# Attention followed by an RWKV channel mix: a new order of steps, tile products in groups, batch 0's query loaded in position halves, and GpSimd's loads held until phi has landed

## The chip, the cores and the metric

The kernel runs on one core of one Trainium2 chip. The metric is the device time of one execution in microseconds (us). A core has five engines with instruction streams of their own: TensorE (PE, matrix products; its weight loads are listed apart as PEld), VectorE (DVE), ScalarE (ACT), GpSimd (POOL) and SyncE (SP). Data come in and go out through DMA queues, into which ACT, POOL and SP put transfers. Engines wait for one another on semaphores.

## The reference

Eight batches of eight heads, 576 positions of 64 features, and 32 slots. Attention goes through the slots:

```python
a = exp(phi - max)                       # phi: 8 x 8 x 576 x 32
a = a / (sum(a, axis=2) + 1e-09)         # softmax over the positions
k_m = einsum('bhsm,bhsd->bhmd', a, k)
v_m = einsum('bhsm,bhsd->bhmd', a, v)
attn = softmax(scale * q @ k_m^T)        # over the 32 slots
attn_out = attn @ v_m
```

The heads are then put side by side (x: 8 x 576 x 512), and the channel mix follows, with 512 model and 1024 inner features:

```python
xk = mu_k * x + (1 - mu_k) * x_prev      # x_prev: x one position earlier
xr = mu_r * x + (1 - mu_r) * x_prev
k = maximum(xk @ w_k, 0)
out = sigmoid(xr @ w_r) * (k * k @ w_v)
```

## The kernel before

**An order written out by hand.** `PLAN` (lines 19 to 84) is a list of words that is executed from left to right (lines 785 to 798); each word issues the instructions of one step, so it fixes the order of every engine's stream. A word is `batch:step`, or `kind:name`. Digits behind `@` are the PSUM banks that the step takes, `/a` and `/d` put a step's copy or activation on ScalarE or VectorE. A step with `yield` in it is named several times, once for each of its parts: first the products, later the work on their result.

**Layout.** A partition's row holds nine neighbouring positions: a batch's q, k, v and phi lie as 128 partitions by (4 head pairs, 9, features), and partitions 0 to 63 hold one head of a pair, 64 to 127 the other. "Position j" below is one of these nine. Many products are tile products: 64 rows by 32 columns of TensorE's array or 32 by 64, so that several heads or pairs run beside each other, each with its own weight load; the others use the whole 128 by 128 array.

**Steps of a batch** (`attention`, names of the words in brackets): exponential of phi (`exp`), its sums over positions by a product with ones (`z`), products of that with k and v (`kv`, or `k`, `v`, and for batch 0 `kg0`, `kg1`, `vg0`, `vg1`, two head pairs each; line 315), normalizing (`nk`, `nv`, for batch 0 `h0`, `h1`; lines 340 and 342), transposing the key and value slots (`tk`, `vt`), transposing q on VectorE (`q0`, `q1`; `turn_q`), scores (`s`, line 401), their exponentials (`es..`), the sums over slots (batch 0: `l`, `r`, `y`, a product, a logarithm and an exponential with negative sign on ScalarE, then the weighing; other batches: a fold on VectorE, `fe`, `fs`, `fo`, and `w0`, `w1`).

**Two ways through the channel mix.** Batch 0 mixes first: `mub` brings mu into the tile `mu_m`, `nk0` to `nr1` (`norm_mu`) make the value slots times mu (the tile `vm`), `mk0`, `mk1`, `mr0`, `mr1` (tile products, `mixed`, line 358) make xk and xr for two ranges of positions (`FIRST`), `uk..`, `ur..` copy them out of PSUM (line 546), `c0:..` multiply with w_k (`key`, line 600), `g:0.` with w_r. Batches 1 to 7 multiply the value slots with the weights instead (`Gs`, `G0`: `project`, line 492; `Es`, `E0`: copies of 512 columns out of PSUM, line 498; `D`: a difference, line 501), with weights scaled by mu (`m:`, line 282 on), and the key products then run on attention's weights (`cN:`, `pair_key`, lines 618 to 626). Relu (`r:`) and square (`s:`) follow on ScalarE and VectorE, the gates (`g:`, `t:`), and the products with w_v (`o:`, `value`, lines 742 and 748) with the store (`store`).

**Fillers.** `b:NxM` (`keep_busy`, line 250) issues N products of zeros, 64 M columns wide, that nothing uses; `WARM` is such a call before the first step.

**Loads.** ScalarE's queue loads batch 0's phi (`load_phi`, line 168) and then k in two halves by head pairs (line 180), as f32; two casts each turn k into bf16 (`0:c..`, `cast_k`). Everything else is loaded by GpSimd (`preload`, the words `p:..`, converted on the way to bf16 where the tile has it), in program order: GpSimd waits at a word for the buffer to be free, and what stands behind it waits too. `PRE` lists what GpSimd does before the plan begins: `q:0g`, the first two head pairs of batch 0's query, then `id`, the identity matrix. `p:q:0h` brings the other two.

**Positions of batch 0.** `scores` works in two parts, `s0` for five of the nine position columns and `s1` for four. In the kernel before, `turn_q` puts position 8 into the first column and positions 0 to 7 behind it, two VectorE transposes for each two head pairs; `tokens` (lines 512 to 515) lists which columns `mixed` takes as now and as one position earlier, and `store` (line 708) where a column's tokens go in the output. `HALVES` are the five and the four columns.

Of the kernel before, what the change touches and what calls it, by code (L numbers as in the profile page):

```python
# [83 lines left out]
]  # L84

WARM = (78, 1)

PRE = "q:0g id:"
TAIL = ("o:71", "o:e3a", "o:e3b",)


NJ = 9
# [5 lines left out]
def kernel(  # L98
# [75 lines left out]
    def load_parity(dst, src, r):  # L174
        nc.gpsimd.dma_start(out=dst[r].rearrange("p h j d -> p h (j d)"), in_=rows(src)[r])
# [654 lines left out]
```

## Time and profile before

| what | value |
|---|---|
| time, median of 3 runs | 201.72 us (201.43 to 202.26) |
| the profiled execution | 201.73 us, span 199.8 us, mean granted clock 0.99 |
| VectorE busy | 159.6 us (80%) |
| ScalarE busy | 147.0 us (74%) |
| moved by DMA | 31.96 MB, mean 160 GB/s |
| instructions | 6543 |

The span goes from the first to the last instruction of the profiled execution. The page's views give, for each engine, its busy time and its share in 40 slices of the span; for each DMA queue what it carried; the chain of waits, which is followed back from the last instruction and tells at each moment what the end depended on (rows: start, length, engine, tile, line, number of instructions); and groups of instructions by line, engine and tile (tile written, tile read, shapes, count, busy time, mean ns). A number in square brackets in a timeline is the idle time ahead of an instruction, with what ended it. "issue" in the chain is time in which an engine waited for nothing that the profile shows. Views by window give the length of a stretch, then the busy time and number of TensorE's products, of its weight loads, and of DVE, ACT, POOL, SP, then the granted clock, the DMA share and GB/s.

### The profile page before, as it was taken

The page shows a single profiled execution, that of the slowest core. Times are in us where ns is not written, and L with a number is a line of the kernel's source. Part 1 is how long each engine was busy: PE and PEld are TensorE (multiplying, and loading weights), DVE is VectorE, ACT ScalarE, POOL GpSimd, SP SyncE. Part 2 cuts the span into 40 slices and gives each one's busy share as a digit, 9 for nine tenths or more (in the row PEclk, how much of TensorE's full clock was granted, in tenths as well). Part 3 has the DMA queues.
Part 4 walks back from the last instruction along what each step waited for, and adds up shares of the span by engine and source line. Part 5 has one row for each costly group of instructions (what it writes and reads, how often), then busy time and mean ns, then how long its engine had stood idle before and what let it go on. Part 6 is the DMA issues. An engine that isn't in the chain of part 4 may idle for free.

```text
span 199.8 us, 6543 instructions
## 1 busy us (share of the span) xinstructions
PE 185.4 (93%) x2655; PEld 105.9 (53%) x2676; DVE 159.6 (80%) x352; ACT 147.0 (74%) x350; POOL 29.3 (15%) x44
## 2 busy tenths in 40 slices
PE   8797999999999999799999999999999999999950
PEld 8443665478644457335645565356544663474430
DVE  2245599898988999699989998998989898996430
ACT  2337797889689688499998689898885799795310
POOL 7644323001240103203015000000000000000000
PEclk9999999999999999999999999999999999999996
DMA  5999999999999992999919999034012411032242
GB/s 203 274 204 259 212 207 199 248 229 290 279 209 213 227 321 35 175 268 262 228 22 190 218 248 206 1 98 117 5 53 55 125 37 41 11 89 74 77 114 75
DMA packets 26174, 31.96 MB, mean 160 GB/s; under 512 B 3096, under 2 KB 20768, under 8 KB 26144
## 3 DMA queue, kind: packets, MB, share of 16 engines
q0 software_dynamic: 17376, 20.32, 55.6%
q1 hardware_dynamic: 7408, 9.19, 16.1%
q10 hardware_dynamic: 1360, 2.03, 3.1%
q8 instruction: 21, 0.34, 0.7%
q14 instruction: 9, 0.07, 0.1%
HBM read 38.28 MB, written 9.44 MB: 239 GB/s over the span
## 4 chain that ended last, share of the span: by engine, by line
PE 77%; DVE 7%; ACT 4%; DMA 3%; issue 3%; SPq 1%; ACTq 1%; DVEq 0%
PE pv L748 25%; PE pk L618 7%; PE pk L626 6%; PE pb L626 6%; PE gps L492 5%; PE idle L250 4%; PE kvps L315 3%; PE pv L742 3%; PE pk L600 3%; DMA k0f<-in_k_dram 3%; PE pb L678 3%; PE pr L670 2%; PE pr L678 2%; DVE rl L586 2%; ACT G L498 2%
## 5 line engine op out<-in xcount | busy, mean ns | idle before, releaser
L748 PE MATMUL pv<-wv,sq 128*128 128x512 bf16 (+1 forms) x276 | 59.3, 355 | 1.1 <-issue 0.5
L498 ACT CAST G<-gps 128x512 bf16<-128x512 f32 x75 | 39.5, 620 | 7.6 <-PE gps L492 7.4
L748 PEld LDWEIGHTS <-sq 128*128 128x128 bf16 x288 | 26.8, 98 | 29.4 <-issue 4.3
L754 DVE SCALAR_TENSOR_TENSOR o<-sg,pv 128x512 f32<-128x512 f32 (+3 forms) x41 | 24.8, 616 | 9.8 <-PE pv L748 5.4
L626 PEld LDWEIGHTS <-G 128*128 128x128 bf16 x224 | 21.3, 97 | 8.0 <-issue 0.9
L626 PE MATMUL pk<-diff,G 128*128 128x288 bf16 x112 | 22.9, 286 | 0.0
L626 PE MATMUL pb<-diff,G 128*128 128x288 bf16 x112 | 22.9, 286 | 0.0
L592 DVE TENSOR_TENSOR sq<-rl 128x576 bf16<-128x576 bf16 (+2 forms) x49 | 20.7, 438 | 1.8 <-ACT rl L584 0.7
L622 ACT COPY pb<-pk 128x288 f32<-128x288 f32 x43 | 16.6, 397 | 6.2 <-PE pk L618 4.6
L618 PE MATMUL pk<-atn,G 128*128 128x288 bf16 x112 | 20.3, 286 | 0.1
L647 ACT ACTIVATE sg<-pr 128x512 f32<-128x512 f32 x22 | 13.1, 606 | 7.8 <-PE pr L700 4.0
L584 ACT ACTIVATE rl<-pk 128x288 bf16<-128x288 f32 (+2 forms) x39 | 16.0, 414 | 3.7 <-PE pk L626 2.0
L584 ACT ACTIVATE rl<-pb 128x288 bf16<-128x288 f32 x36 | 14.6, 421 | 3.5 <-PE pb L626 3.3
L250 PE MATMUL idle<-zeros 128*128 128x64 bf16 (+3 forms) x120 | 15.2, 277 | 1.2 <-DVE zeros L181 1.0
L586 DVE TENSOR_SCALAR rl<-pk 128x288 bf16<-128x288 f32 (+2 forms) x33 | 14.6, 449 | 0.7 <-PE pk L626 0.5
L465 DVE TENSOR_TENSOR atn<-e,lz 128x576 bf16<-128x576 bf16 (+2 forms) x18 | 12.1, 689 | 3.3 <-ACT lz L437 3.1
L501 DVE TENSOR_TENSOR G<-G 128x1024 bf16<-128x1024 bf16 x21 | 14.1, 685 | 0.6 <-ACT G L498 0.4
L618 PEld LDWEIGHTS <-G 128*128 128x128 bf16 x112 | 10.6, 98 | 5.5
L590 ACT ACTIVATE sq<-rl 128x576 bf16<-128x576 bf16 (+2 forms) x23 | 12.3, 559 | 0.4 <-DVE rl L586 0.3
L295 ACT ACTIVATE em<-ph 128x1152 bf16<-128x1152 f32 (+1 forms) x9 | 9.6, 1071 | 1.6 <-DMA ph<-in_phi_dram 1.6
L382 DVE STREAM_TRANSPOSE qT<-q 128x576 uint32<-128x576 uint32 x14 | 10.6, 766 | 0.0
L415 ACT ACTIVATE e<-scps 128x288 bf16<-128x288 f32 x28 | 9.4, 424 | 1.4 <-PE scps L401 1.4
(100 smaller groups left out, 279.2 us busy)
## 6 DMA issues: line engine op xcount, KB each, us to landing
out_dram<-o SPq DMA_DIRECT2D x134, 64.0 KB, 2.8
ph<-in_phi_dram POOLq DMA_DIRECT2D x7, 576.0 KB, 13.6
kv<-in_k_dram POOLq DMA_DIRECT2D x7, 576.0 KB, 14.4
q<-in_q_dram POOLq DMA_DIRECT2D x7, 576.0 KB, 15.4
kv<-in_v_dram POOLq DMA_DIRECT2D x7, 576.0 KB, 12.8
k0f<-in_k_dram ACTq DMA_DIRECT2D x2, 576.0 KB, 7.0
wv<-in_moe_w_v_dram POOLq DMA_DIRECT2D x2, 512.0 KB, 20.1
ph<-in_phi_dram ACTq DMA_DIRECT2D x1, 576.0 KB, 4.5
```

The costliest lines, as they stand in the source:

```text
L250: nc.tensor.matmul(ps.rearrange("p (a b) -> p a b", b=64), lhsT=zeros, rhs=zeros[:, :64].unsqueeze(1).to_broadcast([128, blocks, 64]), sta ...
L498: return lambda: copier()(g_tile()[:, v, c, GCOLS[i]], st["gps", v, i][c])
L501: return lambda: nc.vector.tensor_sub(g_tile()[:, 1, :, GCOLS[i]], g_tile()[:, 2, :, GCOLS[i]], g_tile()[:, 0, :, GCOLS[i]])
L584: nc.scalar.activation(rl, ps, AF.Relu, scale=HALF ** 0.5)
L586: nc.vector.tensor_scalar(rl, ps, 0.0, HALF ** 0.5, op0=AL.max, op1=AL.mult)
L592: nc.vector.tensor_mul(dst, rl, rl)
L618: nc.tensor.matmul(pa, lhsT=st["G"][:, 2, c, f], rhs=st["at"][:, c, :NP], start=c == 0, stop=False, skip_group_check=True)
L622: copier()(pb, pa)
L626: nc.tensor.matmul(ps, lhsT=st["G"][:, v, c, f], rhs=st["d"][:, kind, c], start=False, stop=c == 1, skip_group_check=True)
L647: nc.scalar.activation(gated[name], ps, AF.Tanh, scale=0.5)
L748: nc.tensor.matmul(pv[:, cols], lhsT=sq[:, fi, lo:lo + 128], rhs=wv_sb[:, fi, cols], start=(fi == 0), stop=(fi == NF - 1))
L754: nc.vector.scalar_tensor_tensor(o[:, cols], in0=gated[name][:, cols], scalar=1.0, in1=pv[:, cols], op0=AL.add, op1=AL.mult)
```

## The change

Four things change, in one diff.

- `PLAN` is a new order of the same steps, with other banks and some other engines for copies. Steps with tile products stand more often next to each other: from the first key product on, TensorE's stream changes between tile shapes 61 times where it did 71 times. The fillers are others: 78 of 64 columns, 30 of 512, 9 of 256, and one each of 320, 384 and 448 before; 46 of 512, 4 of 320, 2 of 384, one of 448 and one of 256 after. TensorE's stream has 5214 instructions in place of 5346. Of the copies of 512 columns (line 498) ScalarE has 76 and VectorE 8 (75 and 9 before); the four scalings of w_r go from VectorE to ScalarE.
- `PRE` becomes `id: after: q:0b`. `after` is a new step: GpSimd copies one element of batch 0's phi into the tile `mark`, so it and all that GpSimd loads behind it wait until phi has landed. `WARM` becomes ten fillers of 512 columns.
- Batch 0's query is loaded in position halves: `a` is the first five positions of all head pairs, `b` the other four. `load_parity` is gone. `turn_q` makes one transpose for each half, `q0` for five positions, `q1` for four, and leaves the positions in their order; `tokens` and `store` are adapted to that. `s1` (positions 5 to 8) now stands before `s0`. The first mixing is still `mk0`, from the half of five columns: it makes the tokens of positions 1 to 4 (0 to 3 before).
- `TAIL` (stores that use two queues) names `o:70` in place of `o:71`.

The core of the diff; the plan's first lines, where the order around the start can be followed:

```diff
-    "0:exp0 0:c01/d 0:c00/a 0:exp1 b:7x8@7 b:1x5@7 0:z@0 0:z 0:mub@1 0:mub p:q:0h 0:kg0@02 0:c11/d 0:q1 0:c10/a",
-    "b:10x8@7 0:kg1 0:h1/a 0:h0/a b:3x8@7 b:1x4@7 0:tk@0 0:q0 p:v:0h p:v:0g 0:tk b:2x8@7 0:s0@0123 0:es00 b:1x4@7",
-    "0:vg1@45 0:es10 b:1x7@7 0:l00@6 0:l00 b:1x6@7 0:s1@0123 b:1x4@7 0:l10@6 0:es11 p:wk:0-2 0:r00 0:y00 0:vg0",
-    "b:1x4@3 0:mu@2 0:mu 0:l10 0:l11@7 p:wk:4-8 0:es01 p:wk:2-4 b:1x8@3 b:1x8@6 0:l01@0 p:phi:1 0:nk0 0:nk1 0:r10",
-    "0:y10 0:l01 b:3x8@6 b:1x4@6 0:mk0@2130 0:l11 0:nr1 p:k:1 p:q:1 0:r01 0:r11 0:nr0 0:y01 0:y11 b:3x8@6 0:mk1@4576",
-    "0:uk01/a 0:uk00/a c0:6a@0 c0:5a@1 0:uk11/d 0:uk10/a 0:mr0@2347 0:ur01/d b:1x4@6 c0:6b@5 c0:3b@6 c0:4b@3 c0:0a@7",
...
+    "0:c01/a 0:mu@0 0:exp1 0:c00/d 0:exp0 0:mub@1 0:c10/d b:10x8@7 b:1x6@7 0:kg0@23 0:z@4 0:z 0:c11/a b:1x5@7 0:kg1",
+    "0:h0/a 0:h1/a b:3x8@7 b:1x5@7 0:tk@2 0:q1 0:tk b:4x8@7 b:1x5@7 0:s1@2345 0:es11 b:2x8@7 b:1x6@7 0:l11@6 0:l11",
+    "0:es01 0:mub b:3x8@4 b:1x7@6 0:l01@1 p:q:0a p:v:0g 0:l01 0:vg0@72 0:q0 p:v:0h 0:s0@3451 0:es10 b:2x8@6 b:1x4@6",
+    "0:l10@1 0:vg1 0:nk0 0:es00 0:l00@3 0:r01 0:y01 0:r11 0:mu p:phi:1 0:l10 0:r10 0:y11 0:y10 0:l00 0:r00 0:y00",
+    "0:nk1 b:3x8@6 b:8x8@1 b:1x5@1 0:mk0@0456 p:wk:4-8 p:wk:2-4 p:wk:0-2 p:v:1 0:tb 0:nr1 0:nr0 b:1x8@1 0:mk1@1327",
+    "0:uk01/a 0:uk00/a 0:mr1@4605 0:uk10/d c0:7a@1 p:k:1 0:ur11/d 1:exp c0:5a@2 m:k1/d 0:uk11/a c0:2b@5 c0:2b/d",
...
-WARM = (78, 1)
-
-PRE = "q:0g id:"
-TAIL = ("o:71", "o:e3a", "o:e3b",)
+WARM = (10, 8)
+
+PRE = "id: after: q:0b"
+TAIL = ("o:70", "o:e3a", "o:e3b",)
...
+    mark = const.tile([1, 1], F32, name="mark")
...
-    def load_parity(dst, src, r):
-        nc.gpsimd.dma_start(out=dst[r].rearrange("p h j d -> p h (j d)"), in_=rows(src)[r])
...
+        elif what == "after":
+            nc.gpsimd.tensor_copy(mark, loads[0][:1, 0, 0, :1])
...
-                if part[1:] in ("g", "h"):
+                if part[1:] in ("a", "b"):
+                    js = HALVES["ab".index(part[1])]
+                    js = slice(js.start // QR, js.stop // QR)
+                    nc.gpsimd.dma_start(out=dst[:, :, js].rearrange("p h j d -> p h (j d)"),
+                                        in_=rows(src)[:, :, js.start * D:js.stop * D])
+                elif part[1:] in ("g", "h"):
...
-        def turn_q(gs):
+        def turn_q(gs, js=slice(0, NJ)):
 
             def go():
-                dst = q_tile()[:, gs]
-                src = qs[b % 2][:, gs.start * NJ:gs.stop * NJ]
-                if b:
...
-                nc.vector.transpose(dst[:, :, PB:], src[:, :, :(NJ - 1) * PB])
-                nc.vector.transpose(dst[:, :, :PB], src[:, :, (NJ - 1) * PB:])
+                cols = slice(js.start * PB, js.stop * PB)
+                dst = q_tile()[:, gs].rearrange("p g n h -> p g (n h)").bitcast(U32)[:, :, cols]
+                src = qs[b % 2].rearrange("p (g n) d -> p g (n d)", n=NJ)[:, gs].bitcast(U32)[:, :, cols]
+                nc.vector.transpose(dst, src)
             return go
...
-            ([(0, 4 * QR, QR)], [(QR, 4 * QR, QR), (1, QR, 0)]),
-            ([(4 * QR, 8 * QR, 5 * QR), (8 * QR, S, 0)], [(4 * QR, S, 4 * QR)]),
+            ([(0, 4 * QR, QR)], [(0, 4 * QR, 0)]),
+            ([(4 * QR, 8 * QR, 5 * QR), (8 * QR, S, 0)], [(4 * QR, 8 * QR, 4 * QR), (8 * QR + 1, S, 8 * QR)]),
...
-            steps[f"q{i}"] = turn_q(slice(2 * i, 2 * i + 2))
+            steps[f"q{i}"] = turn_q(slice(2 * i, 2 * i + 2)) if b else turn_q(slice(0, HH), (slice(0, 5), slice(5, NJ))[i])
```

Further down the diff is the plan. Around the places that the prediction names, the plan of batch 1 reads as follows before and after (words from several lines, in order):

```diff
-1:exp ... 1:z ... 1:k@12 ... 1:tk ... 1:s@2451 ... g:03 ... g:01 g:00 ... 1:v@45 g:02 1:vt 1:G02 ... 1:Gs2 1:Gs1 ... 1:G01 ... 1:G00 ... 1:Gs0
+1:exp ... 1:z ... 1:v@56 ... 1:vt ... 0:mr0 ... 1:Gs1@30 1:k@25 1:G01@46 ... 1:G00 ... 1:tk ... 1:Gs0@54 ... 1:q0 1:q1 ... 1:s@3456 ... 1:Gs2 ... g:01 g:03 g:00 ... g:02
```

The tiles that a key or gate product covers, the arithmetic and the stores' sizes are as before.

More of the change, by code (lines that the diff above doesn't have):

```diff
@@ L211, in preload @@
                 src = {"q": q, "k": k, "v": v}[what][n]
-                if part[1:] in ("g", "h"):
+                if part[1:] in ("a", "b"):
[4 more added lines that the diff above has]
+                elif part[1:] in ("g", "h"):
                     gs = slice(0, 2) if part[1] == "g" else slice(2, 4)
                     nc.gpsimd.dma_start(out=dst[:, gs].rearrange("p h j d -> p h (j d)"), in_=rows(src)[:, gs])
-                elif part[1:]:
-                    load_parity(dst, src, ROWS["ab".index(part[1])])
                 else:
@@ L373, in q_tile @@
             return st["qT"]
-        def turn_q(gs):
+        def turn_q(gs, js=slice(0, NJ)):
             def go():
-                dst = q_tile()[:, gs]
-                src = qs[b % 2][:, gs.start * NJ:gs.stop * NJ]
-                if b:
-                    dst, src = dst.rearrange("p g n h -> p (g n h)"), src.rearrange("p n d -> p (n d)")
-                    nc.vector.transpose(dst.bitcast(U32), src.bitcast(U32))
-                    return
-                src = src.rearrange("p (g n) d -> p g (n d)", n=NJ).bitcast(U32)
-                dst = dst.rearrange("p g n h -> p g (n h)").bitcast(U32)
-                nc.vector.transpose(dst[:, :, PB:], src[:, :, :(NJ - 1) * PB])
-                nc.vector.transpose(dst[:, :, :PB], src[:, :, (NJ - 1) * PB:])
+                cols = slice(js.start * PB, js.stop * PB)
+                dst = q_tile()[:, gs].rearrange("p g n h -> p g (n h)").bitcast(U32)[:, :, cols]
+                src = qs[b % 2].rearrange("p (g n) d -> p g (n d)", n=NJ)[:, gs].bitcast(U32)[:, :, cols]
+                nc.vector.transpose(dst, src)
             return go
@@ L712, in store @@
                 if b == 0:
-                    for r, (j, p) in enumerate(((4, 0), (8, PB))):
+                    for r, (j, p) in enumerate(((5, 0), (0, PB))):
                         parts.append((out[0].rearrange("(p j) d -> j p d", j=NJ)[j, p:p + PB], r * PB, PB))
@@ L723, in store @@
                 n = min(QR - p, lo + 128 - at)
-                parts.append((out[0].rearrange("(p j) d -> j p d", j=NJ)[j, p:p + n], at - lo, n))
+                parts.append((out[0].rearrange("(p j) d -> j p d", j=NJ)[(j + 1) % NJ, p:p + n], at - lo, n))
                 at += n
```

116 rows, old and new, of the table PLAN are left out of this document.

## The prediction

> **What bounds the kernel now.** I read the page first (spans, slices, queues, chain), then the chain of waits in order of time, then windows around its two holes, then the head's timeline.
>
> ```profile
> span 199.8 us, 6543 instructions
> PE 185.4 (93%) x2655; PEld 105.9 (53%) x2676; DVE 159.6 (80%) x352; ACT 147.0 (74%) x350; POOL 29.3 (15%) x44
> PE   8797999999999999799999999999999999999950
> q8 instruction: 21, 0.34, 0.7%
> PE 77%; DVE 7%; ACT 4%; DMA 3%; issue 3%; SPq 1%; ACTq 1%; DVEq 0%
> ```
>
> TensorE is the bound: 93% busy, 77% of the chain. Its work is the same in both kernels, so what counts is when the dense part begins, what is lost in it, and filler. The chain shows the places:
>
> ```profile
> 9.49 2.26 PE idle L250 x10
> 13.86 0.29 PE scps L401 x29
> 18.93 1.22 issue
> 21.75 0.98 PE pk L600 x8
> 22.73 0.36 PE mxps L358 x24
> 44.56 0.87 PE pv L748 x8
> 53.80 0.98 PE pv L748 x8
> 74.48 1.73 PE pv L748 x8
> 80.49 1.15 issue
> 131.14 1.83 PE pv L748 x8
> ```
>
> Until 21.75 (first key product) TensorE mostly waits and runs filler; after it the only large hole is 1.15 us at 80.49, charged to "issue", that is to nothing that an engine or a data load did. The four pv rows give the price of going from tile products to full ones: eight matmuls take 0.87 after a full product and 0.98 after 64x32 ones, and, twice as wide, 1.73 and 1.83. So a change of tile shape costs about 0.10 us.
>
> What are the two "issue" holes? Queue q8 carries instructions, 0.34 MB in 21 pieces (row: pieces, MB, share), 16 KB each. TensorE's 2655 + 2676 instructions over 21 are 254 each.
>
> ```profile
> 14.30:20.15 5.85, 4.58 (x130) 2.24 (x129) 2.75 (x9) 4.41 (x16) 2.50 (x3) 1.00 1.25 253
> 20.15:81.63 61.48, 59.21 (x1017) 36.88 (x1023) 54.12 (x124) 50.67 (x121) 12.56 (x17) 1.00 1.11 219
> 77.26:81.63 4.37, 3.23 (x151) 2.31 (x141) 3.44 (x8) 3.38 (x13) 2.78 (x4) 1.00 0.60 82
> ```
>
> Columns: window, length, then busy time and count of TensorE matmuls and weight loads first, DMA share and GB/s last. Between the ends of the holes lie 2040 instructions, eight times 255: both holes end on a piece boundary. Before each, a full piece went by unusually fast, 259 instructions in 5.85 us and 292 in 4.37. My reading is that TensorE used its instructions up before the next piece was there; estimate of the least time for a piece: 5.8 us while loads fill the queues (share 1.25), some 4 where they don't (0.60). Tile products consume instructions fastest.
>
> The Trainium skill (Runtime: NRT & Kernel Launch, Terms) also has instructions refilled in 16 KiB blocks, into a store of 32 to 128 KiB. With a store that large one dense piece would not stop the engine; the two holes above say it did.
>
> **Dense part: what the new placement takes away.** The built programs' orders were counted from the first key product on. Changes of tile shape go from 71 to 61: 10 x 0.10 = -1.0 us (between -0.5, if half were hidden by waits, and -1.0). Four fillers of 256 columns go; eight key products of that width take 0.98 with one shape change in it (row at 21.75), so 0.11 each, -0.44. One of the four token-mixing products moves ahead of the first key: -0.36 (row at 22.73; its sibling is as large). The hole at 80.49 goes if no piece there is dense: -1.15; the new order has 15 us of work in the piece that ends near it. The piece-by-piece sum of TensorE work, at these rates, finds two others: the piece from the end of batch 1's value products to its `Gs0` (72 key/value products, 28 of the projections, 16 mixing) has 3.7 us of work, at about 30 us, where loads run; it would stop up to 2.1, but its waits on ScalarE and VectorE cover part: I take +0.8 (0 to 2.0). And one near 75 us with 4.8 us of work (`3:kv`, transposes, scores): +0.4 (0 to 1.0).
>
> ScalarE and VectorE keep their load (75 to 76 and 9 to 8 of the 512-column projection copies, four mwr scalings to ScalarE); they are not full on average (74%, 80%), and the tail's TensorE order holds the same products, so I cost both at nothing; if the cover is thin, it is in the range.
>
> **Head: loads.**
>
> ```profile
> 5.21 0.68 ACT L295 ACTIVATE em<-ph 128x576 bf16<-128x576 f32 x1 [1.64 <-DMA ph<-in_phi_dram]
> 6.78 0.67 ACT L300 CAST kv<-k0f 128x576 bf16<-128x576 f32 x1 [0.89 <-DMA k0f<-in_k_dram]
> 10.17 0.67 ACT L300 CAST kv<-k0f 128x576 bf16<-128x576 f32 x1 [2.13 <-DMA k0f<-in_k_dram]
> 11.02 0.71 DVE L386 STREAM_TRANSPOSE qT<-q 128x512 uint32<-128x512 uint32 x1 [0.29 <-DMA q<-in_q_dram]
> 2.00:3.00 1.00, 1.00 (x23) 1.00 (x21) 0.22 (x3) 0.71 (x1) 0.93 (x4) 1.00 0.80 227
> 3.00:4.00 1.00, 1.00 (x23) 1.00 (x21) 0.77 (x7) 0.57 (x1) 1.00 (x2) 1.00 1.04 357
> 4.00:5.00 1.00, 1.00 (x25) 1.00 (x23) 0.00 (x1) 0.00 (x0) 1.00 (x3) 1.00 1.06 410
> 5.00:6.00 1.00, 0.94 (x8) 0.39 (x5) 0.00 (x0) 0.68 (x1) 1.00 (x2) 1.00 1.12 297
> ```
>
> phi (0.59 MB) lands at 5.2, k's halves (0.59 MB each) at 6.8 and 10.1. Up to 5.0 about 1.0 MB went by, phi and 0.4 of k, at 410 GB/s in the end; then GpSimd's loads join and the rate drops to 297. The new `after` step puts a GpSimd copy that waits for phi ahead of all GpSimd loads. phi itself gains nothing. k's remaining 0.75 MB at 410 takes 1.8 us: second half landed at about 7.3 instead of 10.1, the first at 6.2.
>
> Behind the waiting copy stand all software loads: first `q:0b`. The copy has no row; memsets of GpSimd took 0.1 to 0.3, I take 0.2, so the first issue is at 5.4. When does it land?
>
> ```profile
> DMA to landing us min/median/max: 6.3/8.4/20.4
> q<-in_q_dram POOLq DMA_DIRECT2D x2, 288.0 KB, 8.3
> ```
>
> At most 8.3 later (the half loads of before, which shared the engines with k); at least 4/9 of 6.3, the fastest whole query, so 2.8. k is through at 7.3 and the queues are then empty: nearer the low end, 3.5, landing 8.9. The Trainium skill (DMA: Bandwidth & Descriptors, Anatomy of one DMA) gives a software load about 2.0 us plus its bytes at 436 GB/s; by it the half lands 2.6 us after issue, and the sum stays as it is. The later loads follow as one stream with the same bytes: the weights land some 1 to 2 us either way of before, ahead of use.
>
> **Head: chain.**
>
> ```profile
> 12.21 0.63 ACT L340 ACTIVATE kbd<-kvps,rz 128x128 bf16<-128x128 f32 x2 [1.37 <-PE kvps L315]
> 13.36 0.29 DVE L368 COPY kmT<-ktps 128x256 bf16<-128x256 bf16 x1 [0.78 <-PE ktps L364]
> 14.30 0.89 ACT L420 ACTIVATE e<-scps 128x160 bf16<-128x160 f32 x4 [1.46 <-PE scps L401]
> 15.21 0.44 ACT L432 ACTIVATE lz<-zps 128x320 f32<-128x320 f32 x1
> 18.23 0.72 ACT L437 ACTIVATE lz<-lz 128x256 f32<-128x256 f32 x2
> 20.55 1.65 ACT L546 CAST x0T<-mxps 128x256 bf16<-128x256 f32 x5 [1.59 <-PE mxps L358]
> L292 ACT ACT_TABLE_LOAD x1 | 1.3, 1283 | 0.0
> L295 ACT ACTIVATE em<-ph 128x1152 bf16<-128x1152 f32 x7 | 8.3, 1182 | 0.0
> ```
>
> ScalarE now casts k's first half before both exponentials: 6.2 + 0.67 + 2 x 0.68 = 8.2, then the key products of two of the four head pairs, the sums, the other two pairs: done at 9.6 (before 12.1). Normalizing 0.63, transposing and copying 0.8 (12.84 to 13.65 in the rows): 11.1; filler of about 1.0 follows, scores at 11.8 instead of 13.86. Two microseconds won, and mostly lost again. The query's second set waits behind `mu_m` on VectorE and on TensorE behind filler, two sums and value products: 14.9. Then ScalarE runs in a row: exponentials 0.89, two reciprocals 0.72, two pairs of log and reciprocal 1.8, from 15.4 to 18.8. Only then is the first mixing ready, since its positions are the half that is scored last (before, the half scored first). Weighing and vm on VectorE bring it to 19.9; the table load (1.28), moved ahead of the casts, ends at 20.1 and is hidden by that. Four casts at 0.33, the mixing `mr1` that needs their banks, the first key at 22.2: +0.5 against 21.75 (from -0.7, if the loads run faster and logs overlap, to +1.3). Next `c0:2b` needs `uk11`, which stands behind the 1.18 us exponential of batch 1 on ScalarE: 22.2 + 0.9 of keys against 23.6, +0.5 (0 to 1.0). The 78 narrow warm-up matmuls become 10 wide ones; both end before k lands, nothing.
>
> **Sum:** -1.0 - 0.44 - 0.36 - 1.15 + 0.8 + 0.4 + 0.5 + 0.5 = -0.75. The profiled run took 201.73 (199.8 span and 1.9 around it; median 201.72), so 201.0. All low ends: -1.0 - 0.44 - 0.36 - 1.15 - 0.7 = -3.65, 198.1; all high: -0.5 - 0.44 - 0.36 - 1.15 + 2.0 + 1.0 + 1.3 + 1.0 = +2.85, 204.6.
>
> **Rivals.**
> 1. The head's gain arrives: pieces do not stop, `uk11` is ready, first key no later than before. Without +0.8, +0.5, +0.5: 199.2. For it: 2 us earlier scores, k's idle queues. Against: ScalarE's row of logs.
> 2. Slower through instructions: dense pieces stop in full, 2.1 and 1.0 in place of 0.8 and 0.4, and the head's piece with the first scores (4.8 us of work) stops 0.5 net: +2.4, 203.4. It decides wherever a piece has less than 5.8 us of work and loads run. For it: both holes of before. Against: waits in these pieces hide part, and the queue may be emptier.
> 3. Slower through the wait for phi: `q:0b` needs the 8.3 us of the rows, lands at 13.7, transposed 14.4, kmT queued behind it 14.7, scores 14.9, three late; the second set two late. About +2.5, 203.5. It decides once the half lands after 11.0. Against: those rows shared the engines. By the skill's price above it does not occur.
> 4. The wait does not do what it says: k's second half still lands near 10.1, because something other than GpSimd's loads slows it. Key products end at 11.4, 1.8 late against my chain: about 202.6. Against: the drop from 410 to 297 GB/s.
>
> **How the numbers follow.** Forecast 201.0 at 0.33; rival 1 0.32, rival 2 0.18, rival 3 0.12, rival 4 0.05. About 0.5% (1.0 us) is what this measurement can tell: faster means under 200.7, slower over 202.7. Faster: rival 1 and a third of the forecast, 0.43. Slower: rivals 2 and 3 nearly whole, part of 4: 0.32. Same: the rest, 0.25. The range 198.4 to 204.4 holds the rivals and trims the extremes; the forecast's own is 200.0 to 202.0.
>
> **What would show it.** k's second cast at about 7.4; first scores at 11.8; first mixing at 19.9; first key at 22.2; no "issue" hole near 80, a smaller one near 34 and perhaps near 76. I am wrong if the first key comes before 21 or after 24, or if holes of more than 3 us in all stand behind TensorE in the dense part.

## The result and the profile after

The changed kernel takes 202.98 us (median of 20 runs, 201.04 to 204.91), the kernel before 201.48 (20 runs, 200.68 to 202.50): ratio 1.0063, 95% interval 1.0040 to 1.0086. It is slower by 0.6%; the forecast was 201.0, faster. Ratios here and below come from comparisons that leave out runs over 1.5% above a kernel's fastest, so that they can lie under the ratio of the medians, by up to 0.9% (a_no_after).

The profiled execution of the changed kernel took 201.04 us, as long as the shortest of its runs. So the profile shows where the change gains and loses, but not what makes most runs 2 us longer; that took experiments. First the page of the changed kernel (span, engines, TensorE's slices, instruction pieces, chain):

```profile
span 198.9 us, 6428 instructions
PE 187.0 (94%) x2610; PEld 104.0 (52%) x2610; DVE 157.7 (79%) x348; ACT 149.3 (75%) x352; POOL 29.6 (15%) x45
PE   8995999799999999999999999999999999999980
...
q8 instruction: 20, 0.33, 0.7%
...
PE 82%; DMA 7%; DVE 5%; issue 2%; ACT 1%; POOL 0%; DVEq 0%
```

From the first key product on, TensorE has one thin place only, the 7 in the eighth slice, and its instructions come in 20 pieces in place of 21. But the head has a thinner one, the 5 in the fourth slice, and the chain (start, length, what) tells why. In the kernel before it leaves the loads at 6.76 us, with k's first half; here it stays with loads, one behind the other, until 17.39:

```profile
0.74 4.32 DMA ph<-in_phi_dram
...
5.23 4.91 DMA q<-in_q_dram
...
10.16 0.72 DVE qT L384
...
11.18 0.73 POOL q L215
11.91 5.48 DMA kv<-in_v_dram
...
17.43 0.45 PE kvps L318 x36
...
35.38 0.66 issue
```

The last row is a part of the stop behind the thin eighth slice (1.43 us from 34.60 on). The query's second half (`q:0a`) is issued only at 11.18, behind the transpose of the first, and v behind it. Three rows from timelines of the changed kernel (start, length, engine, what; in brackets idle time and its releaser) give the wait, the load it delays and the first key product; a last one its last product:

```profile
11.18 0.74 POOL L215 DMA_DIRECT2D q<-in_q_dram  x1 [5.08 <-DVE qT L384]
...
17.43 0.45 PE L318 MATMUL kvps<-kv,em 64*32 64x64 bf16 x36 [2.23 <-DMA kv<-in_v_dram]
...
24.61 1.68 PE L597 MATMUL pk<-x0T,wk 128*128 128x256 bf16 x11
...
192.90 0.84 PE L739 MATMUL pv<-wv,sq 128*32 128x192 bf16 x32 [0.73 <-ACT sg L644]
```

And of the kernel before, the same two landmarks:

```profile
21.68 1.05 PE L600 MATMUL pk<-x0T,wk 128*128 128x256 bf16 x8
...
192.28 0.84 PE L742 MATMUL pv<-wv,sq 128*32 128x192 bf16 x32 [0.28 <-ACT sg L647]
```

That splits the two profiled spans in three:

| stretch, us | before | after | difference |
|---|---|---|---|
| start to first key product | 21.68 | 24.61 | +2.93 |
| first key to end of last product | 171.44 | 169.13 | -2.31 |
| last product to end of span | 6.67 | 5.21 | -1.46 |

The sum, -0.84, is the difference of the spans (198.95 and 199.79, which the page rounds). The medians say +1.5. Three things had to be explained: a head 2.9 us later, a tail 1.5 us shorter, and the 2 us between the profiled run and the median.

### The profile page after: what moved, and what is told of

Same layout as the page of the kernel before. It is cut to its first block, busy times and chain, and to the rows that moved or that the text cites. A ratio compares the mean times of both kernels' runs of the same rounds, so it can differ in the third digit from the quotient of the medians.

```text
span 198.9 us, 6428 instructions
## 1 busy us (share of the span) xinstructions
PE 187.0 (94%) x2610; PEld 104.0 (52%) x2610; DVE 157.7 (79%) x348; ACT 149.3 (75%) x352; POOL 29.6 (15%) x45
## 4 chain that ended last, share of the span: by engine, by line
PE 82%; DMA 7%; DVE 5%; issue 2%; ACT 1%; POOL 0%; DVEq 0%
PE pv L745 27%; PE pk L623 7%; PE pk L615 7%; PE pb L623 7%; PE gps L489 5%; PE pv L739 4%; PE pk L597 4%; PE pr L675 3%; PE pr L667 3%; PE pb L675 3%; PE kvps L318 3%; DMA kv<-in_v_dram 3%; DMA q<-in_q_dram 2%; DMA ph<-in_phi_dram 2%; PE pr L697 2%; PE idle L253 2%
## 5 line engine op out<-in xcount | busy, mean ns | idle before, releaser
L745 PE MATMUL pv<-wv,sq 128*128 128x512 bf16 (+1 forms) x288 | 60.1, 356 | 0.0
L495 ACT CAST G<-gps 128x512 bf16<-128x512 f32 x76 | 40.4, 606 | 4.7 <-PE gps L489 4.4
L581 ACT ACTIVATE rl<-pk 128x288 bf16<-128x288 f32 (+2 forms) x42 | 17.2, 422 | 5.7 <-PE pk L597 3.0
L619 ACT COPY pb<-pk 128x288 f32<-128x288 f32 x40 | 15.8, 410 | 6.7 <-PE pk L615 5.6
L253 PE MATMUL idle<-zeros 128*128 128x512 bf16 (+4 forms) x54 | 15.8, 416 | 1.3 <-DVE zeros L179 1.0
L384 DVE STREAM_TRANSPOSE qT<-q 128x576 uint32<-128x576 uint32 (+2 forms) x16 | 12.1, 765 | 3.7 <-DMA q<-in_q_dram 3.7
L583 DVE TENSOR_SCALAR rl<-pk 128x288 bf16<-128x288 f32 (+2 forms) x30 | 13.3, 454 | 2.0 <-PE pk L597 1.0
L644 ACT ACTIVATE sg<-pb 128x512 f32<-128x512 f32 x14 | 8.5, 610 | 7.7 <-PE pr L697 6.1
L583 DVE TENSOR_SCALAR rl<-pb 128x288 bf16<-128x288 f32 x21 | 9.3, 452 | 1.5 <-PE pb L623 1.4
```

What stands on the lines that cost most here:

```text
L253: nc.tensor.matmul(ps.rearrange("p (a b) -> p a b", b=64), lhsT=zeros, rhs=zeros[:, :64].unsqueeze(1).to_broadcast([128, blocks, 64]), sta ...
L495: return lambda: copier()(g_tile()[:, v, c, GCOLS[i]], st["gps", v, i][c])
L581: nc.scalar.activation(rl, ps, AF.Relu, scale=HALF ** 0.5)
L583: nc.vector.tensor_scalar(rl, ps, 0.0, HALF ** 0.5, op0=AL.max, op1=AL.mult)
L619: copier()(pb, pa)
L644: nc.scalar.activation(gated[name], ps, AF.Tanh, scale=0.5)
```

## The experiments

Times are medians; ratios are to the kernel before on the same chip, with 95% intervals.

| kernel | edit | us | ratio |
|---|---|---|---|
| a_again | the changed kernel once more | 202.52 | 1.0047 (1.0011 to 1.0082) |
| a_q_apart | query halves in two tiles | 199.60 | 0.9888 (0.9836 to 0.9940) |
| a_no_after | no copy that waits for phi | 202.82 | 0.9976 (0.9934 to 1.0017) |
| b_after | before, with that copy | 201.78 | 1.0007 (0.9970 to 1.0044) |
| a_fill | ten fillers in the hole at 15 us | 203.23 | 1.0108 (1.0067 to 1.0148) |
| qa_warm38 | a_q_apart, 56 instructions more | 200.69 | 0.9949 (0.9912 to 0.9985) |
| qa_warm110 | a_q_apart, 200 more | 198.42 | 0.9862 (0.9824 to 0.9900) |
| b_tail70 | before, with the new TAIL | 200.75 | 0.9984 (0.9957 to 1.0010) |
| a_short | short fillers ahead of kg0 | 201.06 | 0.9982 (0.9954 to 1.0011) |
| qa_short | a_q_apart, the same | 199.77 | 0.9918 (0.9887 to 0.9949) |
| qa_best | qa_warm110 and short fillers | 197.37 | 0.9807 (0.9777 to 0.9837) |
| qa_no_after | a_q_apart without the copy | 198.61 | 0.9872 (0.9839 to 0.9904) |
| b_warm10 | before, with the new WARM | 200.31 | 0.9939 (0.9894 to 0.9985) |
| qa_split | qa_best, 34 more changes of shape | 203.46 | 1.0089 (1.0057 to 1.0120) |

### The second half's wait

```diff
+    q0 = {w: const.tile([128, HH, n, D], BF16, name="q0" + w) for w, n in (("a", 5), ("b", 4))}
...
-                    nc.gpsimd.dma_start(out=dst[:, :, js].rearrange("p h j d -> p h (j d)"),
+                    nc.gpsimd.dma_start(out=q0[part[1]].rearrange("p h j d -> p h (j d)"),
```

The two halves write different columns of one tile, interleaved by head pair, yet the load of one waits for the transpose that reads the other. In two tiles it doesn't.

> Batch 0's query halves lie in two tiles of their own, so that the load of the second half no longer waits for the transpose of the first. Theory (this wait sets the head): the second half is issued at about 6.1 us in place of 11.2, lands before 11, v lands before 14 in place of 17.4, the first key product at 21.5 to 22.5 in place of 24.6; time about 2.0 to 2.5 us below the changed kernel's. Rival (the transfers are bound by the queues anyway): second half issued early, but v lands within 1 us of 17.4 and the first key within 0.7 of 24.6.

Timeline of this kernel:

```profile
5.15 0.88 POOL L216 DMA_DIRECT2D q0b<-in_q_dram  x1
6.02 0.75 POOL L216 DMA_DIRECT2D q0a<-in_q_dram  x1
...
14.70 0.45 PE L319 MATMUL kvps<-kv,em 64*32 64x64 bf16 x36
...
22.35 0.83 PE L599 MATMUL pk<-x0T,wk 128*128 128x256 bf16 x6
```

Issued at 6.02, no stop for v any more, first key product at 22.35 in place of 24.61: this one wait cost 2.3 us. The time falls from 1.0063 (1.0047 in a_again, on this chip) to 0.9888 of the kernel before, below both kernels.

### The wait for phi

> The changed kernel without the copy that waits for phi: the query's first half is issued at about 1.4 us. Theory (the copy speeds k up but nothing that lasts): k's second half is cast at about 9.5 in place of 7.9 to 8.2 us, the first scores come 1 to 1.5 us later, the second half of the query is still issued only after the transpose, and the first key comes within 0.7 us of 24.6: time as the changed kernel's to 0.7. Rival (the copy is what costs): first key 1.5 us or more earlier, time down by as much.

> The kernel before with the copy that waits for phi ahead of its first query load, and no other edit. Theory (the wait alone is worth little either way): k's second half lands about 7.3 in place of 10.1 us, the query's halves near 9 to 11 us; time within 1.0 us of the kernel before. Rival (the wait speeds the head up): first key product at 20.5 or earlier in place of 21.75, time down by 1 us or more. Other rival (it delays all software loads): first key 1 us or more later.

> The kernel with the query's halves in two tiles, without the copy that waits for phi. Theory (the copy is worth little, since k's second half is cast only 0.6 us earlier with it, and by then TensorE runs fillers): time within 0.7 us of 199.6. Rival (the copy, now that nothing else holds the query up, brings the head forward): first key product 1 us or more later without it, time 200.6 or more.

In the kernel before the copy changes nothing (1.0007); with the halves in two tiles no gain shows either (0.9888 with it, 0.9872 without; the intervals overlap). It does what it says: k's second cast starts at 8.23 us on ScalarE with it, 8.83 without. But TensorE runs fillers until then, so nobody gains from the 0.6 us. a_no_after can't be read for this: its runs go from 199.7 to 204.3 us, the first key of its profile came at 25.14, and windows of its profile (length; busy time and count of PE, PEld, DVE, ACT, POOL; granted clock, DMA share, GB/s) show why:

```profile
15.00:16.00 1.00, 0.00 (x0) 0.00 (x0) 0.84 (x1) 0.32 (x1) 1.00 (x2) 1.00 1.25 197
...
17.00:18.00 1.00, 1.00 (x34) 0.38 (x27) 0.00 (x0) 0.58 (x4) 0.75 (x2) 0.68 1.17 370
18.00:19.00 1.00, 0.94 (x23) 0.35 (x25) 0.00 (x0) 1.00 (x5) 0.59 (x1) 0.50 0.97 329
...
20.00:21.00 1.00, 1.00 (x4) 0.40 (x3) 1.00 (x5) 0.95 (x3) 0.76 (x1) 0.62 1.26 215
```

The wait for v (1.6 us, 14.90 to 16.51) is followed by 3.4 us at half clock (17.36 to 20.77, by the trace's record of the clock). In the changed kernel's own profile 2.2 us of the same wait had no such consequence. Whether the copy costs something stays open: without it the first value products, which wait for v, start at 16.51 in place of 17.43, and the two shortest runs, 199.74 and 200.13, are shorter than all 32 of the changed kernel.

### Why most runs are longer than the profiled one

> The changed kernel once more. Its shown profile is its shortest run (201.0 us where the median is 203.0), with the first key product at 24.6 us. Theory: the head is the same each time and the 2 us between runs lie behind the first key product, where TensorE's instructions run out (holes of over 0.6 us charged to issue, more than the two of 0.66 and 0.64 us at 35 and 44 us); first key within 24.2 to 25.0. Rival: the loads at the start vary, and the first key product comes 1 us or more later in a run near the median.

The second profile fell on the shortest run again (200.84 us, first key 24.59), so it settles neither theory. The fall of the clock suggested covering the wait:

```diff
-... 0:l01 0:vg0@72 ...
+... 0:l01 b:10x8@6 0:vg0@72 ...
```

> The changed kernel with ten more fillers of 512 columns ahead of batch 0's first value products, where TensorE stood idle for 2.2 us (15.2 to 17.4 us) until v landed. Nothing else changes, v lands as late as before. Theory (the idle stretch lets the clock fall to half in most executions, for 3.3 us, as in the profile without the copy, and this is what sets the median 2 us above the profiled run): no execution has a drop of the clock ahead of the last products, median 1.0 to 2.0 us below the changed kernel's, near 201.0, with a narrower spread. Rival (the spread comes from elsewhere): median within 0.5 us of the changed kernel's or above it by the fillers' 0 to 0.3 us.

The theory fell: 203.23, no gain. But this profile caught a long run (204.67), and its timeline shows what the short ones hide. The eleven fillers ahead of the first key products `kg0`, in a_fill:

```profile
6.63 4.55 PE L253 MATMUL idle<-zeros 128*128 128x512 bf16 x11
11.12 0.45 PE L318 MATMUL kvps<-kv,em 64*32 64x64 bf16 x36
```

and in the profile of the changed kernel:

```profile
6.37 2.71 PE L253 MATMUL idle<-zeros 128*128 128x512 bf16 x11
9.01 0.45 PE L318 MATMUL kvps<-kv,em 64*32 64x64 bf16 x36
```

4.55 us against 2.71 for the same instructions: TensorE starts at half pace (0.427 us from one filler of 512 columns to the next, later 0.216) and is released at some time that differs from execution to execution. Where the spacing changes, the trace's record of the granted clock begins: at 6.0 us in the changed kernel, at 10.4 in a_fill. Released late, the fillers outlast the wait that they were put in for, and `kg0` comes 2.1 us later. The loads follow it: on VectorE the transpose `q1` stands behind the reciprocal of the sums, which come behind `kg0`, so `q:0a` is issued at 13.00 in place of 11.18, v lands at 19.05 in place of 17.39, and the first key product comes at 26.59 in place of 24.61. The rest of a_fill's extra length lies behind the first key: its stop at 35.9 us took 2.07 us, and the clock fell to half for 3.4 us at 37.7.

```diff
-... 0:c10/d b:10x8@7 b:1x6@7 0:kg0@23 ...
+... 0:c10/d b:10x1@7 b:1x6@7 0:kg0@23 ...
```

> The changed kernel with the ten fillers of 512 columns ahead of the first key products (kg0) cut to 64 columns each: as many instructions, 4480 columns less. In the profiles these fillers ran at 1.2 columns per ns until TensorE's clock was released (between 3.6 and over 11 us after the start, another time in each profile) and at 2.4 behind it; eleven of them took 2.71 us in the changed kernel's profile and 4.55 us in the profile with fillers in the hole, and the first key products came at 9.0 and 11.1 us. Theory (most executions are released late, so the wide fillers hold up the head by 2 us, and this makes the median 2 us longer than the profiled run): first key products at 9.0 or earlier, median near 201.0 (200.5 to 201.6), narrower spread. Rival (the spread comes from the stop for instructions at 34 us and the fall of the clock behind it): median within 0.6 us of the changed kernel's.

> The kernel with the query's halves in two tiles, with the same short fillers. Theory: the late release costs here too, so the median falls by 0.5 to 1.2 us against the wide ones (199.6), to 198.4 to 199.1. Rival: no change beyond 0.4.

a_short: 201.06, as expected, and 0.9982 of before; the wide fillers cost the median about 1.5 us. Its profile was released only at 13.7 us, and the first key product came at 24.64 all the same. With the halves in two tiles the shorter fillers gave nothing (0.9918 against 0.9888). The profile of qa_short (199.88, near the median) shows what stood against them:

```profile
10.40 1.95 PE L254 MATMUL idle<-zeros 128*128 128x512 bf16 x4
...
12.41 1.78 PE L254 MATMUL idle<-zeros 128*128 128x512 bf16 x5
...
23.82 1.81 PE L599 MATMUL pk<-x0T,wk 128*128 128x256 bf16 x12
```

It was released at 13.3 us, and the nine wide fillers that are left behind the key products ran at half pace for the most part (1.95 and 1.78 us; 1.17 and 1.38 in the changed kernel's profile), so the first key came at 23.82, 1.5 us later than in a_q_apart, released at 5.0. Whether the other runs of qa_short were released as late is not known. With the instruction pieces moved as well, the shorter fillers gave 1.0 us (qa_best against qa_warm110, below).

How often the release is late was not measured. Of the sixteen profiles twelve were released between 3.6 and 7.0 us and four between 9.5 and 13.7, but a run without a profile gives only its span and mean clock. The mean clock alone does not tell the long runs: among a_short's, 0.973 went with 201.0 us and 0.996 with 201.5. In the changed kernel it does go with them (0.996 in the shortest run, 0.974 to 0.989 in the other nineteen), so falls of the clock behind holes may have a part in the 2 us.

### Instructions that come late

> The kernel with the query's halves in two tiles, with 38 warm-up fillers of 128 columns in place of 10 of 512: TensorE's instruction stream gets 56 instructions more at its very start, 4864 columns in place of 5120. Theory (TensorE runs out of instructions at every 254.7th one): the hole at 32.35 us (ahead of a Gs0 step, 1.38 us) moves 56 instructions up the order, to about 30.4 us, into the group of key and value products, and grows to some 2.8 us; the hole of 0.69 us at 87.7 goes; time +0.5 to +1.0 us. Rival (the hole belongs to the step that follows it): it stays ahead of the same step with 1.4 us, and the time stays within 0.4.

> The same kernel with 110 warm-up fillers of 64 columns: 200 instructions more at the start. Theory: the boundaries fall 200 instructions earlier, which leaves holes of about 1.1 us at 17 us (partly in place of fillers), 0.3 at 29.6 and 0.7 at 34.6, and none near 88: together some 1.0 us less on the path; time 0.5 to 1.0 us lower than with ten wide fillers. Rival (holes belong to steps): the hole ahead of Gs0 stays, time within 0.4.

Edit of qa_warm38; qa_warm110 has `(110, 1)` in its place:

```diff
-WARM = (10, 8)
+WARM = (38, 2)
```

TensorE's timeline around the hole, in a_q_apart:

```profile
31.96 0.39 PE L491 MATMUL gps<-wk,vT 64*32 64x512 bf16 x1
33.73 0.41 PE L491 MATMUL gps<-wk,vT 64*32 64x512 bf16 x7 [1.38 <-DVE kmT L372]
```

and in qa_warm38, whose only difference is the number and width of the fillers at the very start (its profiled run, 202.73, is one of its longer ones):

```profile
32.18 0.79 PE L319 MATMUL kvps<-kv,em 64*32 64x64 bf16 x67
35.87 0.21 PE L319 MATMUL kvps<-kv,em 64*32 64x64 bf16 x5 [2.90 <-issue]
```

The hole left the projection, where it sat behind the first of eight products, and moved into the key and value products, behind the 67th of 72; 2.90 us where 2.8 were expected. In both traces the next instruction is the same by number, 1214 among the recorded products and weight loads. The holes of the other kernels stand at such numbers too, whatever the step: at 702 in the kernel before (18.93 us) and in qa_best, at 2742 in the kernel before (80.49 us) and in a_q_apart (87.7 us); 702 is two pieces before 1214, and 2742 six behind it. The profile names VectorE's `kmT` as releaser in the first case; the product doesn't read it. The second hole (87.7 us) is gone in qa_warm38. The steps are innocent: it is a count. The time rises from 0.9888 to 0.9949. With 200 instructions more the only such hole left is one of 0.35 us at 18.6, and the time is 198.42 (0.9862; the interval overlaps with that of a_q_apart), though its fillers held `kg0` up to 10.32.

> The query's halves in two tiles, the short fillers, and 110 warm-up fillers of 64 columns (200 instructions more, which moved the boundaries of TensorE's instruction pieces to places without holes of over 0.4 us behind the first key product). Theory: gains add: first key product at 22.3 to 23.2 in place of 24.3, median 197.0 to 198.0. Rival (the head is bound elsewhere): within 0.4 of 198.4.

Both together, in TensorE's timeline of qa_best:

```profile
8.40 0.45 PE L319 MATMUL kvps<-kv,em 64*32 64x64 bf16 x36
...
22.52 1.81 PE L599 MATMUL pk<-x0T,wk 128*128 128x256 bf16 x12
```

197.37 us, runs from 196.88 to 198.14: 1.9% below the kernel before, 2.5% below the changed one (0.9807 over 1.0063).

### The tail

> The kernel before, with the last stores on two queues for o:70 in place of o:71 (the one word of the change's TAIL). In the profile of before SyncE's stores of o:73 are issued 0.01 us after the landings of ScalarE's two stores of o:71 (192.52 and 194.46 us), and the span ends 6.7 us after the last product; in the changed kernel 5.2. Theory (this queueing is worth 1.5 us): last product to end of span 5.0 to 5.5 us, time 1.2 to 1.6 us below the kernel before. Rival (the order of the last steps makes the difference, not the word): 6.3 us or more from last product to end, time within 0.4.

```diff
-TAIL = ("o:71", "o:e3a", "o:e3b",)
+TAIL = ("o:70", "o:e3a", "o:e3b",)
```

A miss: 7.3 us from the last product to the end, time unchanged. The other candidate was the 21st instruction piece of the kernel before, loaded among its last stores:

```diff
-WARM = (78, 1)
+WARM = (10, 8)
```

> The kernel before with the change's warm-up alone: 10 fillers of 512 columns in place of 78 of 64, which is 136 instructions fewer in TensorE's stream, so 20 pieces in place of 21, and nothing is loaded for it behind 186 us. Theory (a piece loaded among the last stores holds these up, which then hold up SyncE's queue): last product to end of span 5.2 us in place of 6.7. The pieces of the middle fall otherwise too: holes of some 2 us near 15 us (partly in fillers) and 2 to 4 us near 77 in place of 1.2 at 18.9 and 1.15 at 80.5; time within -0.5 to +2.0 of the kernel before. Rival (the order of the last steps sets that stretch): 6.5 us or more from last product to end.

The queues from 188 to 194 us in the kernel before (packets, MB, share; then issues with their median us to landing), and SyncE's and ScalarE's last stores:

```profile
q8 instruction: 1, 0.02, 1.4%
out_dram<-o ACTq DMA_DIRECT2D x2, 64.0 KB, 2.5
...
192.53 5.06 SPq L731 DMA_DIRECT2D out_dram<-o  x8
192.77 1.97 ACTq L731 DMA_DIRECT2D out_dram<-o  x4
```

The same in b_warm10, where no piece is loaded there:

```profile
out_dram<-o ACTq DMA_DIRECT2D x2, 64.0 KB, 1.8
...
192.65 3.59 SPq L731 DMA_DIRECT2D out_dram<-o  x8
192.89 1.74 ACTq L731 DMA_DIRECT2D out_dram<-o  x4
```

The instructions of this stretch are the same to 0.1 us; the eight last issues of SyncE take 5.06 us with the piece and 3.59 without, and last product to end is 6.67 and 5.21. With the piece in between, a store of ScalarE lands 3.3 us after its issue (191.15 to 194.46), and SyncE's next store is issued 0.01 us later. The three profiles with a piece loaded at 192 us (before, b_after, b_tail70) end 6.7 to 7.3 us after the last product; twelve of the thirteen others 5.2, one 5.7. Three of these others have 21 pieces too, but the last is loaded at 187 to 189 us, ahead of the last stores. So the tail's gain in the changed kernel comes from when its last piece is loaded, with 132 instructions fewer, and not from its order. One constant of the change alone makes the kernel before 0.6% faster (0.9939), in spite of a hole that grew from 1.15 to 1.58 us at 78 us.

### The price of a change of shape

```diff
-... 4:G02@34 4:E020/a 4:G00@56 ...
+... 4:G02@34 4:E020/a b:1x1@5 4:G00@56 ...
```

(at 17 places of batches 4 to 7)

> The best kernel so far (query halves in two tiles, short fillers, 110 narrow warm-up fillers; 197.4 us) with 17 fillers of 64 columns put between neighbouring steps of tile products in batches 4 to 7: 34 more changes of tile shape, 34 more instructions. Theory (a change costs 0.093 us and is not hidden): 17 x (2 x 0.093 + 0.03) = 3.7 us more, 200.5 to 201.5. Rival (half of it hides behind waits for copies of earlier products): 1.2 to 2.2 us more, 198.6 to 199.6. Other rival (changes cost next to nothing in place): under 0.8 us more.

203.46 against 197.37: 6.1 us for 34 changes and 17 narrow fillers (5.7 by the ratios, since the two were measured on different chips). Without 0.5 us for the fillers' columns that is 0.16 for a change, but it is not the price of the kernel's own changes. Take the time from one product's start to the next, less the first one's columns at 2.4 per ns. In qa_split's trace 0.11 us are left over from a tile product to the filler and 0.23 from the filler of 64 columns to the next tile product; with the filler's own 0.03 that makes 6.2 us at 17 places. At the kernel's own changes the median is 0.10 in the kernel before (71 changes) and in the changed one (61). So the prediction's 0.10 stands, and what is dear here is the way from a narrow filler to a tile product.

## Why the prediction was wrong

**What bounds the kernel: right. The dense part: its terms right in kind, several sizes off.** Terms of -1.0 (shape), -0.44, -0.36, -1.15, +0.8, +0.4 and +0.5 make -1.25; measured -2.31 in this profile, -1.6 with a_q_apart, which stops for 0.69 us at 87.7. The hole at 80.49 went, and the one expected near 34 us came (1.43; +0.8 taken, up to 2.0). The one near 75 did not; in some profiles 0.7 stood at 88 instead. The stop for `uk11` was 0.2 us, not 0.5. The four fillers of 256 columns took 0.9 us from their starts to the next products' (0.11 to 0.34 each), not 0.44. Two things had no term. Seven of the 71 changes of shape in the kernel before held a short wait besides (0.20 to 0.48 us each by the measure of qa_split, 1.3 us over the 0.10; four more, where the trace lacks a product, are left out), one of the 61 in the changed kernel (0.39): about -1.0. And the wait of the last product, in brackets in the rows above, grew from 0.28 to 0.73 us: +0.45. With these the terms add to -2.3; that is an account of one profile of each kernel, not an experiment.

**Head: the step that failed.** The prediction named what stands behind the waiting copy, and let "the later loads follow as one stream". They don't: `q:0a` carries a wait of its own, for `q1` on VectorE. The query's second set was put at 14.9 and came at 17.81; "first key at 22.2" came at 24.61, later than the 24 that the prediction itself named as a sign of being wrong, and at 22.35 once the wait was gone. So the chain of ScalarE's logarithms was right, and +0.5 became +2.9 by one semaphore. Other steps of the head came later than forecast as well: `q:0b` landed at 10.14 (8.9), k's second cast began at 8.23 (7.4), the first scores at 12.77 (11.8). They did not decide: in a_q_apart `q:0b` landed at 10.22, and the first key still came 0.15 us from the forecast. Rival 3 had the right size for a wrong reason: `q:0b` took 4.9 us from issue to landing, not 8.3 (nor the 3.5 of the sum, nor the 2.6 that the prediction worked out beside it).

**"Both end before k lands, nothing":** true of the warm-up, not of the fillers behind it. Their durations were taken from a profile in which the clock had been released (the row at 9.49 of the chain: 0.23 us each). Released at 10.4 us they last 4.55 us, and a_short puts about 1.5 us of the median on them.

**The tail, "at nothing":** -1.5 us. The prediction used queue q8 to explain holes in TensorE and did not ask what else is in the queues when its last piece comes.

For the profiled run the corrected terms add: +2.9 - 2.3 - 1.5 = -0.9. That this run, 201.04, met the forecast of 201.0 is luck: +0.5, -1.25 and 0 make nearly the same sum. The median adds the late release, and what falls of the clock behind holes cost; their shares are open.

## What to carry to other kernels

Ask of each load in a changed order which semaphore it waits for in the built program, not only which one was meant to be added: two column ranges of one tile may be one object to the dependency tracker. Size fillers by the slowest clock, since a filler that outlasts its cover is on the path. Where tile products are dense, the number of instructions ahead of a place decides whether TensorE stops there; a constant at the start moved the time by 0.6% here, down in b_warm10 and up in qa_warm38, and two orders are compared fairly only with this phase in view.

## What was not expected of the hardware

- Fillers at the start run at 1.2 columns per ns until a release that came between 3.6 us (qa_split) and 13.7 us (a_short). TensorE's first filler starts at 0.99. The column of the granted clock shows 1.00 throughout, since the trace holds no record of the clock from before the release. The Trainium skill (TensorE: Matmul & The Clock Gate, Part 1: The HAM clock gate) puts the release about 4 us into sustained activity, 500 ns either way, by a window that runs free of the kernel. The releases here came 2.7 to 12.7 us behind the first filler, so the late ones are outside that.
- The clock fell to half for 3.4 us each time with stops of 1.6 (a_no_after), 2.1 (a_fill) and 2.9 us (qa_warm38), and did not with one of 2.2 us in the changed kernel. The 3.4 us are the window that the same page gives.
- Crossing a 16 KB boundary of instructions cost up to 2.9 us. The Trainium skill (Runtime: NRT & Kernel Launch, Instruction fetch mechanics) calls that cost mostly hidden; with tile products under load it is not.
